# Decode attention over a long cache: thirty units as a hardware loop, each engine in the written order

## The chip, the cores and the metric

The kernel runs on one core of a Trainium2 chip. The metric is the device time of one execution in microseconds (us); runs of one kernel agree within about a tenth of a per cent here.

## The reference

Two branches, mixed by a gate. Cut to what matters:

```python
x = A_x                                              # [2, 1, 1024], bf16
g = sigmoid((x * gate_w).sum(-1, keepdims=True))
# A: attention of one query per head over a cache of 16384 keys
q = (x @ wq) in heads                                # 32 heads of 128
p = softmax(q @ k_cache^T * 128 ** -0.5)             # k_cache, v_cache: [2, 32, 16384, 128]
a = (p @ v_cache) in one row @ wo                    # wo: [4096, 1024]
# B: a small MLP on x (with Sq = 1 the shifted branch hs is zero)
b = x + gelu(layernorm(x) @ w3) @ w4
out = g * a + (1 - g) * b
```

Nearly all of the bytes are the two caches: 2 x 32 x 16384 x 128 x 2 bytes each, 537 MB together. The weights add some 36 MB.

## The kernel before, in words

Two heads of one batch row make a *unit*: 16 pairs of heads (`HP`) times 2 rows (`b`) are 32 units. A unit loads 8.4 MB of K and 8.4 MB of V, each as one DMA of 128 rows of 65,536 bytes. SBUF holds five cells of half such a load in `mem`: K of row 0 takes cells 0 and 1, K of row 1 cells 1 and 2 (they share cell 1), V cells 3 and 4. So a load of K can be issued only when the first half of the K before it, in cell 1, has been used up, and a load of V only when the V before it has.

All large loads are issued by SP's queue, in this order in each pair: K of row 0, V of the row before, K of row 1, V of row 0, with the waits that follow from the shared cells.

What a unit computes:

- `score_first`, `score_second`: K is turned chunk by chunk (8 chunks) by DVE into one of two `KT` buffers (L420), and PE adds the scores up in PSUM, 8 matmuls per chunk (L426). POOL prepares the weights `qw` (L357). The chunks in cell 1 are taken first, so that the next load of K (`load_k`, L108) can start after them.
- `softmax_a`, `softmax_b`: DVE turns the scores (L447) and takes the maximum (L449); ACT (L451) and PE (L457) spread it; ACT takes the exponentials (L464); PE sums them (L475), DVE inverts (L476).
- `pv`: 64 matmuls with V (L492), after which the next V can be loaded (`load_v`, L115).
- `pv_end`: ACT scales (L505), PE gathers (L517), DVE writes the pair's `oT` (L525). After the second row, `project` multiplies `oT` by the pair's two heads of `wo` (L378), held in `wo_pair`, and `load_wo` (L370) fetches the next 512 KB into the same buffer when `project` is through.

The program is software-pipelined by hand: scores of one unit come before the product with V of the unit before. `odd_rest(hp)` finishes unit (hp, 1) and `even_unit(hp + 1)` does unit (hp + 1, 0) and the first half of (hp + 1, 1). They are written out 15 times, which is units 1 to 30; `last_unit` does the rest with its own load of `wo` (`wo_last`, L614) and V in five pieces. A framework schedules this straight-line code: it may move an instruction ahead of others on its engine where the data allow, and it sets the semaphores.

In the trace PE's order differs from the written one in one place: in even units the matmul L457 of `softmax_b` stands before `project`.

Of the kernel before, what the change touches and what calls it, by code (L numbers as in the profile page):

```python
# [23 lines left out]
def kernel(  # L24
# [15 lines left out]
    nc = tc.nc  # L40
# [10 lines left out]
    HP = H // 2  # L51
# [28 lines left out]
    def region(cell, elements, offset=0):  # L80
        at = cell * CELL + offset
        return mem[:, at : at + elements]
# [20 lines left out]
    def cache_rows(cache, hp, b):  # L103
        two = cache[b, bass.ds(2 * hp, 2)]
        return two.rearrange("h s d -> (h s) d").rearrange("(p j) d -> p (j d)", p=P)

    def load_k(hp, b):
        nc.sync.dma_start(out=region(K_CELL[b], NJ * Dh), in_=cache_rows(A_k_cache, hp, b))  # L108

    def load_v(hp, b, cell=V_CELL, pieces=(NJ,)):  # L110
        rows = cache_rows(A_v_cache, hp, b)
        j = 0
        for n in pieces:
            at = slice(j * Dh, (j + n) * Dh)
            nc.sync.dma_start(out=region(cell, NJ * Dh)[:, at], in_=rows[:, at])  # L115
            j += n
# [251 lines left out]
    def load_wo(hp):  # L368
        rows = A_wo[bass.ds(hp * 2 * Dh, 2 * Dh)]
        nc.sync.dma_start(  # L370
            out=wo_pair[:].rearrange("p t n -> p (t n)"),
            in_=rows.rearrange("(p t) n -> p (t n)", p=P),
        )

    def project(oT, weight, last):
        for t in range(2):
            for g in range(Q4):
                nc.tensor.matmul(  # L378
                    arow[QP * g : QP * g + B, :],
                    lhsT=oT[:, t, :],  # L380
                    rhs=weight[:, t, g * G1 : (g + 1) * G1],
                    start=False,
                    stop=(last and t == 1),
                    skip_group_check=True,
                )
# [51 lines left out]
    def score_first(hp, b):  # L437
        write_qw(hp, b)
        score_chunks(b, halves[1 - b], True, False)

    def score_second(b):
        score_chunks(b, halves[b], False, True)

    def softmax_a(b):
        S = S_tiles[b]
        st = ppool.tile([P, GT, QP], FP32, name="St")
        nc.vector.transpose(out=st[:].rearrange("p j r -> p (j r)"), in_=S[:])  # L447
        m = stat.tile([P, 1], FP32, name="m")
        nc.vector.tensor_reduce(out=m[:], in_=st[:, :, 0:NG], axis=AX.XY, op=ALU.max)  # L449
        Dm = ppool.tile([P, P], FP32, name="Dm")  # L450
        nc.scalar.activation(out=Dm[:], in_=ident_s[:], func=ACTF.Copy, scale=m[:, 0:1])  # L451
        st_tiles[b] = (st, Dm)

    def softmax_b(b, by_head=False):
        st, Dm = st_tiles.pop(b)
        R_ps = misc_psum([P, P])
        nc.tensor.matmul(R_ps[:], lhsT=ones_f[:], rhs=Dm[:], start=True, stop=True)  # L457
        nb = stat.tile([P, 1], FP32, name="nb")
        rs = stat.tile([P, 1], FP32, name="rs")
        parts = [slice(e * HALF, (e + 1) * HALF) for e in range(2)]  # L460
        for rows in parts:
            nc.vector.tensor_reduce(out=nb[rows], in_=R_ps[rows, rows], axis=AX.X, op=ALU.min)  # L462
        for e, rows in enumerate(parts):
            nc.scalar.activation(  # L464
                out=pts[b][rows, :, e, :].rearrange("p (m a) k -> p a k m", a=GT // 4),
                in_=st[rows, :, 0:NG].rearrange("p (a k) m -> p a k m", k=4),
                func=ACTF.Exp,
                bias=nb[rows],
                scale=scale,
                accum_out=rs[rows],  # L470
            )
        tot_ps = misc_psum([P, 2])
        rinv = rinvs[b]
        if not by_head:
            nc.tensor.matmul(tot_ps[:, 0:1], lhsT=lmat[:], rhs=rs[:], start=True, stop=True)  # L475
            nc.vector.reciprocal(out=rinv[:, 0:1], in_=tot_ps[:, 0:1])  # L476
        else:
            rs2 = stat.tile([P, 2], FP32, name="rs2")
            nc.vector.tensor_scalar(
                out=rs2[:], in0=hm2[:], scalar1=rs[:, 0:1], scalar2=None, op0=ALU.mult  # L480
            )
            nc.tensor.matmul(tot_ps[:], lhsT=ones_f[:], rhs=rs2[:], start=True, stop=True)
            nc.vector.reciprocal(out=rinv[:], in_=tot_ps[:])
            nc.vector.tensor_scalar(
                out=rinv[:], in0=rinv[:], scalar1=g_rep[:, b : b + 1], scalar2=None, op0=ALU.mult
            )

    def pv(b, g0=0, g1=NJ // 4, ng=NJ // 4, cell=V_CELL):
        V = view(cell)
        for g in range(g0, g1):  # L490
            q = g % Q4
            nc.tensor.matmul(  # L492
                oacc[b][QP * q : QP * q + 8, :],
                lhsT=pts[b][:, g].rearrange("p h k -> p (h k)"),
                rhs=V[:, 4 * g : 4 * g + 4, :].rearrange("p j d -> p (j d)"),
                start=(g < Q4),
                stop=(g >= ng - Q4),
            )
# [12 lines left out]
    def pv_end(b):  # L511
        osb = pv_rows(b, True)[:].rearrange("p (k d t) -> p k t d", k=4, t=2)
        ot = misc_psum([P, 2])
        for t in range(2):
            for k in range(4):
                for h in range(2):
                    nc.tensor.matmul(  # L517
                        ot[h * HALF : (h + 1) * HALF, t : t + 1],
                        lhsT=osb[:, k, t, :],
                        rhs=lane[:, k + 4 * h : k + 4 * h + 1],  # L520
                        start=(k == 0 and t == 0),
                        stop=(k == 3),
                        skip_group_check=True,
                    )
        nc.vector.tensor_scalar(  # L525
            out=oT[:, :, b], in0=ot[:], scalar1=g_rep[:, b : b + 1], scalar2=None, op0=ALU.mult
        )
# [26 lines left out]
    def pv_end_apart(b):  # L554
        osb = pv_rows(b, True)
        ot = misc_psum([P, 2])
        for k in range(4):
            nc.tensor.matmul(
                ot[:], lhsT=osb[:, k * Dh : (k + 1) * Dh], rhs=lane[:, k : k + 5 : 4],
                start=(k == 0), stop=(k == 3),  # L560
            )
        nc.vector.tensor_scalar(
            out=OTl[:, :, b], in0=ot[:], scalar1=g_rep[:, b : b + 1], scalar2=None, op0=ALU.mult
        )
# [14 lines left out]
    softmax_b(0)  # L579

    def odd_rest(hp):
        load_k(hp + 1, 0)
        score_second(1)
        softmax_a(1)
        pv(0)
        load_v(hp, 1)
        pv_end(0)
        softmax_b(1)

    def even_unit(hp):  # L590
        score_first(hp, 0)
        load_k(hp, 1)
        score_second(0)
        softmax_a(0)
        pv(1)
        load_v(hp, 0)
        pv_end(1)
        project(oT, wo_pair, False)
        load_wo(hp)
        softmax_b(0)  # L600
        score_first(hp, 1)

    load_wo(0)
    score_first(0, 1)

    def last_unit(hp):
        V_LAST = 0
        load_v(hp, 1, V_LAST, PIECES)
        score_second(1)
        wo_last = region(V_CELL, 2 * D).rearrange("p (h n) -> p h n", h=2)  # L610
        softmax_a(1)
        pv(0)
        pv_end_apart(0)
        nc.sync.dma_start(  # L614
            out=wo_last, in_=A_wo[(H - 2) * Dh : H * Dh].rearrange("(h d) n -> d h n", d=Dh)
        )
        softmax_b(1, by_head=True)
        pv_last(1, V_LAST)
        project(OTl, wo_last, True)
        nc.vector.tensor_copy(out=out_row[:], in_=arow[:])  # L620
        rows = out.rearrange("b s (g n) -> (b s) g n", g=Q4)
        for b, queue in enumerate((nc.sync, nc.scalar)):
            queue.dma_start(
                out=rows[b], in_=out_row[:].rearrange("(g k) n -> k g n", k=QP)[b]
            )

    LOOPED = False
    if LOOPED:
        with tc.For_i(0, HP - 1, 1, iteration_sync="reg_based") as i:
            odd_rest(i)  # L630
            even_unit(i + 1)
            with tc.If(i >= HP - 2):
                last_unit(HP - 1)
    else:
        for i in range(HP - 1):
            odd_rest(i)
            even_unit(i + 1)
        last_unit(HP - 1)


# [28 lines left out]
```

## Time and profile before

| | |
|---|---|
| three runs | 1343.05, 1343.83, 1343.95 us; median 1343.83 |
| profiled execution | 1342.64 us, of which the span from the first to the last instruction is 1340.8 us |
| busy | PE 755.4, PEld 329.9, DVE 648.7, ACT 129.6, POOL 12.8 us |
| DMA | 573.05 MB read on SP's queue, 428 GB/s on the mean over the span |
| instruction fetches | 45 packets, 0.74 MB on the queue q8; 10 packets, 0.08 MB on q14 |
| mean granted TensorE clock | 0.783 |

Busy times of engines overlap each other; a share of the span says little about what sets the end. In the queues' rows the last number is the time that their packets took, as a share of the time of all 16 DMA engines. "SPq" in the order of time is an issue of a DMA on SP's queue, not the transfer. A bracket at the end of a row is the idle time of the engine before it and what ended that.

### The profile page before, as it was taken

How to read it: one execution, taken by the hardware profiler on the slowest of the kernel's cores; microseconds unless marked ns; L12 is line 12 of the kernel's file. 1: busy time of each engine (PE TensorE's matmuls, PEld its weight loads, DVE VectorE, ACT ScalarE, POOL GpSimd, SP SyncE). 2: the span in 40 equal slices, each digit the busy share in tenths (PEclk: the TensorE clock that was granted, in tenths of full speed). 3: DMA queues.
4: the chain of work that ended last, by engine and by line, in shares of the span. 5: the costliest groups of instructions: out<-in, count | busy, mean ns of one | idle time of the engine just before them, and what ended most of it. 6: DMA issues, size and time to landing. Idle time of an engine off the chain costs nothing.

```text
span 1340.8 us, 12847 instructions
## 1 busy us (share of the span) xinstructions
PE 755.4 (56%) x5758; PEld 329.9 (25%) x5758; DVE 648.7 (48%) x511; ACT 129.6 (10%) x202; POOL 12.8 (1%) x47
## 2 busy tenths in 40 slices
PE   0466555566545466655546655555664555666456
PEld 0222222222222222222222222222222222222223
DVE  1255544455544445554445554444555434455543
ACT  0100011110011111001111101111100111110011
POOL 0000000000000000000000000000000000000000
PEclk9887777888777788776778877778876777887777
DMA  9999999999999999999999999999999999999997
GB/s 407 433 419 438 436 435 423 437 423 438 431 433 436 427 435 431 428 436 435 427 440 435 429 432 423 436 433 437 425 435 433 426 434 421 438 431 440 421 427 316
DMA packets 13575, 573.88 MB, mean 428 GB/s; under 512 B 1864, under 2 KB 1872, under 8 KB 4432
## 3 DMA queue, kind: packets, MB, share of 16 engines
q1 hardware_dynamic: 13096, 573.05, 99.2%
q8 instruction: 45, 0.74, 0.2%
q10 hardware_dynamic: 424, 0.01, 0.0%
q14 instruction: 10, 0.08, 0.0%
HBM read 573.05 MB, written 0.00 MB: 427 GB/s over the span
## 4 chain that ended last, share of the span: by engine, by line
DMA 72%; DVE 12%; PE 12%; issue 4%; POOL 0%; ACT 0%; ACTq 0%; DVEq 0%
DMA mem<-in_A_k_cache_dram 68%; DVE KT L420 11%; PE S L426 11%; DMA gwT<-in_gate_w_dram 2%; DMA mem<-in_A_wo_dram 1%; PE oacc L194 0%; POOL ln_rstd L265 0%; PE misc L259 0%; DVE spread L165 0%; PE misc L245 0%; DVE turn L204 0%; PE arow L378 0%; PE misc L230 0%; ACTq L85 0%; DVE out_row L620 0%
## 5 line engine op out<-in xcount | busy, mean ns | idle before, releaser
L426 PE MATMUL S<-KT,qw 128*128 128x512 bf16 x2048 | 546.3, 416 | 414.4 <-DVE KT L420 414.1
L420 DVE STREAM_TRANSPOSE KT<-mem 128x2048 f32<-128x2048 f32 x256 | 570.6, 2282 | 320.7 <-DMA mem<-in_A_k_cache_dram 270.9
L426 PEld LDWEIGHTS <-qw 128*128 128x128 bf16 x2048 | 218.5, 107 | 737.3 <-issue 557.3
L492 PE MATMUL oacc<-mem,pt 128*8 128x512 bf16 x2032 | 117.0, 383 | 0.3 <-DMA mem<-in_A_v_cache_dram 0.3
L451 ACT ACTIVATE Dm<-ident_s,m 128x128 f32<-128x128 f32 x32 | 12.9, 403 | 1026.5 <-DVE m L449 1026.5
L464 ACT ACTIVATE pt<-St,nb 64x256 bf16<-64x256 f32 x64 | 89.7, 1401 | 61.7 <-DVE nb L462 60.8
L475 PE MATMUL misc<-rs,lmat 128*128 128x1 f32 x62 | 18.2, 362 | 93.4 <-ACT pt L464 93.4
L525 DVE TENSOR_SCALAR oT<-misc,g_rep 128x2 bf16<-128x2 f32 x30 | 6.7, 222 | 129.1 <-PE misc L517 129.1
L492 PEld LDWEIGHTS <-pt 128*8 128x8 bf16 x2032 | 46.6, 87 | 67.8 <-issue 14.8
L447 DVE STREAM_TRANSPOSE St<-S 128x512 f32<-128x512 f32 x32 | 22.9, 717 | 65.8 <-PE S L426 65.8
L476 DVE RECIPROCAL rinv<-misc 128x1 f32<-128x1 f32 x31 | 5.2, 169 | 102.1 <-PE misc L475 102.1
L517 PE MATMUL misc<-lane,osb 128*64 128x1 f32 x960 | 33.8, 199 | 25.5 <-ACT osb L505 25.5
L517 PEld LDWEIGHTS misc<-lane,osb 128*64 128x64 f32 x960 | 31.3, 138 | 40.7 <-ACT osb L505 40.7
L475 PEld LDWEIGHTS misc<-rs,lmat 128*128 128x128 f32 x62 | 15.5, 311 | 101.2 <-ACT pt L464 101.2
L464 ACT ACTIVATION_READ_ACCUMULATOR pt<-St,nb 64x1 f32 x64 | 30.5, 477 | 0.0
L505 ACT ACTIVATE osb<-oacc,rinv 128x512 f32<-128x512 f32 x31 | 21.3, 687 | 58.0 <-PE oacc L492 58.0
L357 POOL TENSOR_TENSOR qw<-qdu,mask 128x16 bf16<-128x16 bf16 x32 | 8.4, 265 | 1184.7 <-PE S L426 1170.5
L462 DVE TENSOR_REDUCE nb<-misc 64x1 f32<-64x64 f32 x64 | 14.2, 222 | 9.2 <-PE misc L457 8.1
L230 PE MATMUL misc<-zp,ones_f 128*128 128x2 f32 x2 | 0.6, 363 | 31.3 <-DVE zp L228 31.3
L457 PE MATMUL misc<-Dm,ones_f 128*128 128x128 f32 x64 | 15.8, 329 | 0.0
L449 DVE TENSOR_REDUCE m<-St 128x1 f32<-128x256 f32 x32 | 13.4, 420 | 1.1
L457 PEld LDWEIGHTS misc<-Dm,ones_f 128*128 128x128 f32 x64 | 9.6, 189 | 0.7 <-issue 0.2
(95 smaller groups left out, 73.7 us busy)
## 6 DMA issues: line engine op xcount, KB each, us to landing
mem<-in_B_w_dram SPq DMA_DIRECT2D x2, 7168.0 KB, 33.0
wo_pair<-in_A_wo_dram SPq DMA_DIRECT2D x16, 512.0 KB, 32.0
mem<-in_B_w_dram SPq DMA_DIRECT2D x2, 2048.0 KB, 10.2
mem<-in_A_v_cache_dram SPq DMA_DIRECT2D x1, 4096.0 KB, 41.6
mem<-in_A_v_cache_dram SPq DMA_DIRECT2D x1, 2048.0 KB, 30.7
mem<-in_A_v_cache_dram SPq DMA_DIRECT2D x1, 1024.0 KB, 29.3
mem<-in_A_v_cache_dram SPq DMA_DIRECT2D x2, 512.0 KB, 28.4
mem<-in_A_k_cache_dram SPq DMA_DIRECT2D x32, 28.7
```

The costliest lines, as they stand in the source:

```text
L420: nc.vector.transpose(out=kt[:], in_=Kc.rearrange("p j d -> p (j d)").bitcast(FP32))
L426: nc.tensor.matmul(S, lhsT=qw[b][:, v, NG - 1 - m : NG - 1 - m + P], rhs=ktb[:, half * GT : (half + 1) * GT, w, :, e], start=(first and n ...
L447: nc.vector.transpose(out=st[:].rearrange("p j r -> p (j r)"), in_=S[:])
L449: nc.vector.tensor_reduce(out=m[:], in_=st[:, :, 0:NG], axis=AX.XY, op=ALU.max)
L451: nc.scalar.activation(out=Dm[:], in_=ident_s[:], func=ACTF.Copy, scale=m[:, 0:1])
L457: nc.tensor.matmul(R_ps[:], lhsT=ones_f[:], rhs=Dm[:], start=True, stop=True)
L462: nc.vector.tensor_reduce(out=nb[rows], in_=R_ps[rows, rows], axis=AX.X, op=ALU.min)
L464: nc.scalar.activation(out=pts[b][rows, :, e, :].rearrange("p (m a) k -> p a k m", a=GT // 4), in_=st[rows, :, 0:NG].rearrange("p (a k) m ...
L475: nc.tensor.matmul(tot_ps[:, 0:1], lhsT=lmat[:], rhs=rs[:], start=True, stop=True)
L492: nc.tensor.matmul(oacc[b][QP * q : QP * q + 8, :], lhsT=pts[b][:, g].rearrange("p h k -> p (h k)"), rhs=V[:, 4 * g : 4 * g + 4, :].rearra ...
L505: nc.scalar.activation(out=osb[:], in_=oacc[b][:], func=ACTF.Copy, scale=rinvs[b][:, 0:1] if scaled else 1.0,)
L517: nc.tensor.matmul(ot[h * HALF : (h + 1) * HALF, t : t + 1], lhsT=osb[:, k, t, :], rhs=lane[:, k + 4 * h : k + 4 * h + 1], start=(k == 0 a ...
```

## The change

The 15 written-out rounds become a loop of the chip's own, in which every engine runs its part of the body and branches back. Three things come with it:

- The loop is made with `iteration_sync="reg_based"`: the engines don't meet between rounds and semaphores are never set back; a wait in the body compares with a register that its engine raises every round.
- `in_order` chains, for each engine, every instruction of the body to the one before it, without a semaphore, so that the schedule keeps the written order. The last unit, in an `If` in the body that holds in the last round alone, is chained in the same way.
- `load_wo` goes from the end of `even_unit` to the head of `odd_rest`, that is, of the body. The first one, ahead of the loop, goes into the first round, and the sixteenth, whose data nothing reads (the last unit has `wo_last`), is gone.

```diff
     def odd_rest(hp):
+        load_wo(hp)
         load_k(hp + 1, 0)
         score_second(1)
 ...
         project(oT, wo_pair, False)
-        load_wo(hp)
         softmax_b(0)
         score_first(hp, 1)
 
-    load_wo(0)
     score_first(0, 1)
 ...
-    LOOPED = False
-    if LOOPED:
-        with tc.For_i(0, HP - 1, 1, iteration_sync="reg_based") as i:
-            odd_rest(i)
-            even_unit(i + 1)
-            with tc.If(i >= HP - 2):
-                last_unit(HP - 1)
-    else:
-        for i in range(HP - 1):
-            odd_rest(i)
-            even_unit(i + 1)
-        last_unit(HP - 1)
+    def in_order():
+
+        last = {}
+        for ins in nc.cur_bb.bb.instructions:
+            if ins.engine in last:
+                tc.add_manual_dep(
+                    ins,
+                    last[ins.engine].name,
+                    mybir.DependencyInfo(
+                        mybir.DependencyClass.NoSync, mybir.DependencyReason.DATA
+                    ),
+                    reason="in order",
+                )
+            last[ins.engine] = ins
+
+    with tc.For_i(0, HP - 1, 1, iteration_sync="reg_based") as i:
+        odd_rest(i)
+        even_unit(i + 1)
+        in_order()
+        with tc.If(i >= HP - 2):
+            last_unit(HP - 1)
+            in_order()
```

## The prediction

> **What bounds it now.** I read the page first, then the stretches of time, the order of time over one pair of heads and over the end, and the DMA packets themselves.
>
> ```profile
> span 1340.8 us, 12847 instructions
> ...
> PE 755.4 (56%) x5758; PEld 329.9 (25%) x5758; DVE 648.7 (48%) x511; ACT 129.6 (10%) x202; POOL 12.8 (1%) x47
> ...
> DMA  9999999999999999999999999999999999999997
> ...
> q1 hardware_dynamic: 13096, 573.05, 99.2%
> q8 instruction: 45, 0.74, 0.2%
> ```
>
> No compute engine is over 56% busy; the DMA engines are at 9 tenths until the last slice.
>
> ```profile
> core 0: us, PE busy (x) PEld busy (x) DVE busy (x) ACT busy (x) POOL busy (x), PEclk, DMA share, GB/s
> 119.00:1284.00 1165.00, 678.87 (x5013) 294.00 (x5011) 584.20 (x415) 114.39 (x177) 7.70 (x29) 0.78 1.00 432
> 1284.00:1341.00 57.00, 31.71 (x270) 14.63 (x270) 21.09 (x19) 7.00 (x11) 0.00 (x0) 0.73 0.83 355
> ```
>
> In the 1165 us of the thirty units the DMA share is 1.00. A packet of 65,536 bytes takes 2.42 us on its engine and the next begins where it ends. So time there is bytes, not waits; what an engine loses off the DMA counts only past its cover. The cover is seen in one odd unit:
>
> ```profile
> 750.53 0.33 SPq L108 DMA_DIRECT2D mem<-in_A_k_cache_dram  x1
> ...
> 752.75 1.90 PE L426 MATMUL S<-KT,qw 128*128 128x512 bf16 x8 [0.29 <-DVE KT L420]
> ...
> 764.82 0.33 SPq L115 DMA_DIRECT2D mem<-in_A_v_cache_dram  x1
> ...
> 766.69 0.49 PE L457 MATMUL misc<-Dm,ones_f 128*128 128x128 f32 x2
> ...
> 781.34 4.51 DVE L420 STREAM_TRANSPOSE KT<-mem 128x2048 f32<-128x2048 f32 x2 [10.19 <-DMA mem<-in_A_k_cache_dram]
> ```
>
> V is issued at 764.8 while K still runs until 774.5 on the earliest DMA engine and 780.9 on the latest; then DVE sits 10.2 us until K is in.
>
> **A hidden spread.** Each load is eight large packets and one 4-byte packet on each of 16 engines. The 4-byte packets of the load that ended at 166.4 us lie within 1.8 us of each other; of the one that ended at 1018.4, within 7.9: seven engines within 1.8 us of the first, nine 4.1 to 7.9 behind. Over ten rounds (four loads and one wo each) the earliest engine goes from 164.5 to 951.2, 78.67 us a round, and the latest from 166.4 to 957.8, 79.14. What differs is the q8 row: PE's instructions come as 45 packets of 16,384 bytes, one per 256 instructions (11,516 matmuls and weight loads), each 1.07 us on one DMA engine; followed from end to start they take about eight engines in rotation. A buffer is full when its latest engine is done, so those engines pace the kernel, 0.47 us a round behind the bytes.
>
> **The change, part by part.** The sum starts from the profiled execution, 1342.64 us (span 1340.80, 1.84 around it); the median of three runs, 1343.83, is 1.19 above.
>
> *One load of wo less.* It is 512 KB: at 16 x 65,536 bytes per 2.42 us, 1.21 us. It is issued at 1283.77, ahead of the last V pieces:
>
> ```profile
> 1283.77 0.33 SPq L370 DMA_DIRECT2D wo_pair<-in_A_wo_dram  x1
> 1284.15 22.96 SPq L115 DMA_DIRECT2D mem<-in_A_v_cache_dram  x5
> ...
> 1330.67 1.04 PE L492 MATMUL oacc<-mem,pt 128*8 128x512 bf16 x16 [0.34 <-DMA mem<-in_A_v_cache_dram]
> ...
> 1336.87 0.60 PE L378 MATMUL arow<-mem,OTl 128*2 128x256 bf16 x8 [0.70 <-DMA mem<-in_A_wo_dram]
> ```
>
> The end waits for DMA there three times, 0.34, 0.74 (last V piece) and 0.70 us, and the earlier two sum to 1.08 before the compute chain is the end itself: gain 1.1.
>
> *Load of wo at the head.* On SP nothing stands between the old and the new place: V, wo, K, V, K, V, wo is the queue either way, and wo's wait for project (2.35 us each, 35.3 over 15) still ends some 21 us before the next K is issued (729.32, 750.53). Zero; without that cover, a few tenths.
>
> *Written order.* Against the order of time only one pair swaps: the maximum's matmul L457 (728.47) now stands behind project (728.89), which waits for oT. softmax_b starts some 0.8 us later in even units, under DVE's 7.1 us wait for K at 740.0. Zero; uncovered, 15 x 0.8.
>
> *The loop, instructions.* A round is 336 matmuls and 336 weight loads (163 and 172 matmuls in two 39-us stretches): 2.6 packets of 256. The arm with the last unit, jumped over in 14 rounds, holds 236 of each, 1.85 packets. A round's path on PE thus spans about 4.5 packets. If they stay in PE's instruction memory, the loop fetches nothing after its first round. Then the latest DMA engine loses its lag: at least 2.63 / 8 x 1.07 = 0.35, at most 0.47 us a round, over 15 rounds 5.3 to 7.1; I take 6.2. If each round fetches anew the sign turns (first rival). What speaks for staying is the rotation over eight DMA engines, eight packets under way or in place against 4.5 needed; it is inference, and no run here has a loop. [...]
>
> *The loop, waits and branches.* Waits compare with registers, and every engine takes two taken branches a round: over the last unit's arm, and back. No row shows either. Nearest rows: 0.02 to 0.06 us between a KT's end and its matmul; for a missed fetch, 1.25 us (output issue 1337.98 to packet 1339.22) plus none or one large packet of 2.42 plus 1.07: 2.3 to 4.7 us a branch, 9.4 a round. PE's back edge falls after 752.5, ahead of V's issue, whose cover is 774.5 - 764.8 - 1.25 = 8.5 us to the earliest DMA engine and 14.8 to the latest. SP, ACT and POOL have over 20 us between their uses. Zero in the rounds. In the last round the handovers from K's landing (1295.4) to the output are bare: about 25 steps, none to 0.05 each, 0 to 1.2 us; I take 0.7. There a lost fetch would be bare too, 4.7 at most.
>
> *Entering the loop.* SP may have to see the loads ahead of the loop land before it issues its first K in the loop. That K is issued at 118.44 now; the loads land from 124.6 on the earliest engine to 127.7 on the latest. Then the latest engine stands for 1.25 us, the earliest for 127.7 + 1.25 - 124.6 = 4.4, their middle 3, once. Zero to 3; I take 1.5, near the latest engine's.
>
> Sum: 1342.64 - 1.1 - 6.2 + 0.7 + 1.5 = 1337.5; on the median, **1338.7**. With the ends of each term 1335.6 (7.1 saved, nothing paid) to 1346.3 (5.3 saved; 1.2, 4.7 and 3 paid).
>
> **Rivals.**
> *PE's instructions are fetched anew each round: slower.* Place: PE's two taken branches. A path of 4.5 packets with the one ahead at both jumps is 6 a round against 2.63. Spread over eight engines, 6 / 8 x 1.07 = 0.80 us a round against 0.47 now: +5; if a block always comes over the same engine, 1.07 a round, +9. With -1.1, +0.7, +1.5: 1350 to 1354, call it 1350. It decides where fewer than five packets stay in place; the break-even is about 3.5 fetched a round. For it: the 45 packets come one per 256 instructions, as two places used in turn would give as well. Against: the eight engines. [...]
> *As many fetches as now.* 2 to 4 packets a round, say because the arm stays but the body doesn't: only wo is left, minus tail and entry: 1343 to 1345, no change. The rotation speaks no more for this than for a full refetch.
> *A stall past its cover.* Two misses behind a queue as deep as at the start (small packets for gate_w took 29.6 us there) hold PE over 15 us; every us beyond costs 15: 1365 with 1.5 over. In the steady part PE's fetches begin within 7 us of the instruction that crosses the block, so this is unlikely.
>
> **How the numbers follow.** Forecast 0.50, full refetch 0.33, fetches as now 0.10, stall past cover 0.07. A difference under 0.2% (2.7 us) can't be told from none. Of the forecast's 0.50, 0.03 falls within 2.7 us through the entry and tail terms; the case of equal fetches gives 0.08 to no change, 0.02 to slower. So faster 0.47, same 0.11, slower 0.42. The range holds the forecast from its low end (1335.6, with 1 below for the fetches of the other engines, 10 packets now) to the refetch on fixed engines, 1354; left out are the stall case, 0.07, and some of the edges. The forecast's own range is 1334.5 to 1346.3.
>
> **What would show it.** Right: q8 in the changed profile falls from 45 to about 10 packets; q1 falls from 573.05 to 572.53 MB; the spread between the DMA engines' last packets stays under 3 us through the loop; DMA share stays 1.00; SP keeps V, wo, K. Wrong: q8 at 75 or more packets, with the spread growing faster than 0.47 us a round; DMA share under 0.98 in the rounds with SP waiting; PE idle at L426 put down to issue after the first half's matmuls; or a gap in DMA at 120 to 130 us well over 3 us.

## The result and the profile after

The changed kernel takes 1408.37 us (median of 4 runs, 1406.83 to 1413.45) against 1343.44 beside it: 1.049 times the time of before, with a 95% interval of 1.0462 to 1.0519. It is slower by 65 us, 4.6 us for each of the 14 rounds that pass over the last unit. Its four runs lie 0.5% apart, those of the kernel before 0.1%. The forecast was 1338.7 in a range of 1334.5 to 1354; it was wrong, in sign and in size.

The profiled execution took 1406.83 us. Its page, in the rows that answer to those shown of before:

```profile
span 1404.7 us, 14848 instructions
...
DMA  9999999989899998999989898998989999898996
...
q1 hardware_dynamic: 12952, 572.53, 95.3%
q8 instruction: 7, 0.11, 0.0%
...
wo_pair<-in_A_wo_dram SPq DMA_DIRECT2D x15, 512.0 KB, 3.3
```

The last of these rows, in the page of before:

```profile
wo_pair<-in_A_wo_dram SPq DMA_DIRECT2D x16, 512.0 KB, 32.0
```

The part that I forecast a gain from is there: q8 has 7 packets where there were 45, and q1 carries 0.52 MB less. But the DMA row now has an 8 every few slices (a round is 2.4 of them): the DMA engines run dry. The row of wo says where. The median wo now lands 3.3 us after its issue, where it took 32.0 before: it used to stand in a queue of work, and now meets an empty one. The one issued at 729.32 before had its first packet at 753.90; the one issued at 706.12 now has it at 707.19, and its packets, eight of 4,096 bytes on each of the 16 DMA engines at 0.16 us each, are through at 709.10.

From SP's part of the order of time, two rounds (start, duration, engine and line, operation, tile and source):

```profile
672.85 0.33 SPq L115 DMA_DIRECT2D mem<-in_A_v_cache_dram  x1
706.12 0.33 SPq L370 DMA_DIRECT2D wo_pair<-in_A_wo_dram  x1
706.96 0.34 SPq L108 DMA_DIRECT2D mem<-in_A_k_cache_dram  x1
...
756.55 0.33 SPq L115 DMA_DIRECT2D mem<-in_A_v_cache_dram  x1
790.66 0.33 SPq L370 DMA_DIRECT2D wo_pair<-in_A_wo_dram  x1
```

Between V at 672.85, the last issue of one body, and wo at 706.12, the first of the next, SP issues nothing for 33 us. The 4-byte packets that end the load of V land between 703.87 and 704.68 us, and nothing is queued behind it. Before, wo and K went out while V was still on its way:

```profile
726.60 0.33 SPq L115 DMA_DIRECT2D mem<-in_A_v_cache_dram  x1
729.32 0.33 SPq L370 DMA_DIRECT2D wo_pair<-in_A_wo_dram  x1
750.53 0.33 SPq L108 DMA_DIRECT2D mem<-in_A_k_cache_dram  x1
```

There this V's last packets end between 753.9 us on the earliest DMA engine and 760.0 on the latest, so K stood in the queue 3.4 to 9.5 us before them, behind wo. The DMA engines over the edge of the changed kernel, by stretches (the last three columns are granted clock, DMA share and GB/s):

```profile
core 0: us, PE busy (x) PEld busy (x) DVE busy (x) ACT busy (x) POOL busy (x), PEclk, DMA share, GB/s
703.00:709.00 6.00, 5.42 (x24) 2.22 (x23) 4.34 (x2) 0.00 (x0) 0.00 (x0) 1.00 0.47 175
709.00:716.00 7.00, 5.39 (x100) 2.83 (x98) 1.45 (x4) 1.09 (x2) 0.27 (x1) 1.00 0.84 337
716.00:728.00 12.00, 0.59 (x2) 0.53 (x3) 0.52 (x3) 2.81 (x4) 0.00 (x0) 0.51 1.01 437
```

In the thirteen microseconds from 703 to 716 the DMA lost 0.53 x 6 + 0.16 x 7 = 4.3 us; from 716 on it is full. The longest wait of SP's queue (waiting line, what it waited for: us in total, times, longest):

```profile
SPq L645 <- SPq L645: 441.3, 28, 19.6
```

L645 is the `If` around the last unit. SP waits there 28 times, twice in each of the 14 rounds that jump over it, for 441 us, and the row of the profile doesn't say for whom. The records of the trace do. These are SP's records of L645 behind the branch at the edge above: start, operation, and the semaphore that it waits for (`>=`) and then raises (`+=`):

```
673.53 ALU_OP
673.62 EVENT_SEMAPHORE  $S[115]>= $S[115]+=
673.69 ALU_OP
673.76 EVENT_SEMAPHORE  $S[116]>= $S[116]+=
673.83 ALU_OP
673.90 EVENT_SEMAPHORE  $S[117]>= $S[117]+=
673.96 ALU_OP
685.72 EVENT_SEMAPHORE  $S[118]>= $S[118]+=
685.79 ALU_OP
705.07 EVENT_SEMAPHORE  $S[119]>= $S[119]+=
705.14 EVENT_SEMAPHORE  $S[120]>= $S[120]+=
705.21 EVENT_SEMAPHORE  $S[121]>= $S[121]+=
705.28 EVENT_SEMAPHORE  $S[122]>= $S[122]+=
```

The trace has these instructions, eight in each of the 14 rounds (17 ns each once the wait is over):

```profile
L645 SPq EVENT_SEMAPHORE  x112: 17/17/17, 173.8 to 1292.8; - x112
```

By the issues' records, loads take eight semaphores in turn, 115 to 122 in the trace and counted 0 to 7 here. In the body wo has 0, K of row 0 has 1, V of the row before 2, K of row 1 has 3, V of row 0 has 4; the eight DMAs of the arm (V in five pieces, wo_last, two outputs) go on with 5, 6, 7, 0, 1, 2, 3, 4. In each of the 14 rounds that jump over the arm SP raises all eight by hand, as I read it so that they stand as if the arm had run, and the raise waits first: in all 14 rounds that of 3 comes 0.02 us after the last count of K of row 1, and that of 4 comes 0.02 us after the last count of V of row 0. In the edge above, three of them are raised by 673.96, the one of K of row 1 at 685.72 and the one of V of row 0 at 705.07. V's last packet had landed at 704.68, and V's semaphore had its last count at 705.05. Only then come a branch at 705.58, wo at 706.12 and the next K at 706.96. In the 14 rounds it is 33.0 to 34.6 us from V to wo, and 1.9 us from V's last count to the next K: each time, every load that the body had issued had landed before the next body issued one.

### The profile page after: what moved, and what is told of

It is laid out like the page before. It is cut to its first block, busy times and chain, and to the rows that moved or that the text cites. A ratio compares the mean times of both kernels' runs of the same rounds, so it can differ in the third digit from the quotient of the medians.

```text
span 1404.7 us, 14848 instructions
## 1 busy us (share of the span) xinstructions
PE 765.4 (54%) x5758; PEld 334.5 (24%) x5758; DVE 651.5 (46%) x511; ACT 129.6 (9%) x202; POOL 12.8 (1%) x47
## 5 line engine op out<-in xcount | busy, mean ns | idle before, releaser
L426 PE MATMUL S<-KT,qw 128*128 128x512 bf16 x2048 | 553.1, 421 | 437.1 <-DVE KT L420 429.7
L475 PE MATMUL misc<-rs,lmat 128*128 128x1 f32 x62 | 18.2, 362 | 100.7 <-ACT pt L464 55.1
L457 PE MATMUL misc<-Dm,ones_f 128*128 128x128 f32 x64 | 17.4, 357 | 0.0
L457 PEld LDWEIGHTS misc<-Dm,ones_f 128*128 128x128 f32 x64 | 10.7, 210 | 4.1 <-issue 3.9
```

The costliest lines, as they stand in the source:

```text
L426: nc.tensor.matmul(S, lhsT=qw[b][:, v, NG - 1 - m : NG - 1 - m + P], rhs=ktb[:, half * GT : (half + 1) * GT, w, :, e], start=(first and n ...
```

## The experiments

Three theories stood after the result, and the expectations number them so. Theory 1 (landing): this wait of SP on the path past the arm. Theory 2 (edge): what every loop brings, its branch back and its waits on registers. Theory 3 (order): the written order delays the issue of K.

**The last unit behind the loop.** There is no arm here, and so there are no semaphores to raise; the rest of the loop is as changed.

```diff
-        with tc.If(i >= HP - 2):
-            last_unit(HP - 1)
-            in_order()
+    last_unit(HP - 1)
```

> The loop of 15 rounds stays, with the written order and the load of wo at its head; the last unit stands after the loop, so that there is no arm to jump over. Theory 1 (landing): on the path past the arm SP raises the semaphores of the arm's eight loads by hand and waits for each to stand at the value of the last load that used it, so K and V must have landed at each round's edge; the DMA engines run dry some 4.4 us in each of 14 rounds. Without the arm the rounds run at the rate of the bytes, 1336 us, and leaving the loop costs once, since SP sees all loads land there: 1336 + 3 to 10 = 1339 to 1346. Theory 2 (edge): the branch back and the waits on registers cost by themselves, in every round, arm or not: 1400 to 1410. Theory 3 (order): the written order delays K's issue: 1400 to 1410.

It took 1344.55 us (1344.07 to 1346.12), 1.0011 of before [1.0002, 1.0021]. The loss is gone, with the loop, its branch back, the register waits and the written order still there: theories 2 and 3 fall. But it isn't faster than before either. Leaving the loop costs once nearly what each round cost, 0.71 x 5 = 3.6 us of DMA against the 4.3 at the edge above:

```profile
1295.00:1305.00 10.00, 5.38 (x23) 2.07 (x21) 3.93 (x2) 0.00 (x0) 0.00 (x0) 0.99 1.03 446
1305.00:1310.00 5.00, 1.57 (x13) 0.41 (x13) 1.50 (x1) 0.00 (x0) 0.00 (x0) 0.54 0.29 84
```

The DMA share falls to 0.29 for these 5 us. SP stood at L641, the line of the loop, until a V landed, before it issued V of the last unit:

```profile
SPq L641 <- DMA mem<-in_A_v_cache_dram: 8.8, 1, 8.8
```

**One load less in the arm.** V of the last unit in four pieces of 128, 64, 32, 32 columns instead of five; all else as changed. By the count above the arm's seven loads end at semaphore 3, so 4, that of V, is not raised.

```diff
-    PIECES = (128, 64, 32, 16, 16)
+    PIECES = (128, 64, 32, 32)
```

> The changed kernel with the arm's last two V pieces (16 and 16) joined in one of 32, so that the arm has seven loads in place of eight; nothing else. The eight load semaphores go round: wo 0, K 1, V 2, K 3, V 4 in the body, and the arm goes on with 5, 6, 7, 0, 1, 2, 3; the one that falls out is 4, that of the V issued last. Theory 1 (landing): SP waits past the arm for K alone (semaphore 3), which lands some 10 us before SP could issue its next K anyway, and no longer for V: 1335 to 1341, some 68 us less than the changed kernel, from one load joined. Theories 2 and 3: no change but the last piece, 1405 to 1412.

It took 1339.23 us (1338.45 to 1342.51), 0.9974 [0.9964, 0.9983]: 69.1 us less than the change, for two pieces joined in one line of the last unit: 4.9 for each of the 14 rounds that pass the arm. It also beats the kernel before, by 0.3%.

```profile
span 1336.1 us, 14788 instructions
...
DMA  9999999999999999999999999999999999999997
...
q8 instruction: 7, 0.11, 0.0%
```

The row of DMA is at 9 throughout. In its order of time wo goes out 14 us after V and the next K 11 us later, and V is still being read then (its last packets land at 1148.6 to 1150):

```profile
1117.87 0.33 SPq L115 DMA_DIRECT2D mem<-in_A_v_cache_dram  x1
1132.30 0.34 SPq L370 DMA_DIRECT2D wo_pair<-in_A_wo_dram  x1
1143.77 0.33 SPq L108 DMA_DIRECT2D mem<-in_A_k_cache_dram  x1
```

SP still stands at L645, once a round instead of twice, now for K alone:

```profile
SPq L645 <- SPq L645: 165.7, 15, 12.5
```

These 165.7 us of waiting cost nothing, because K lands a whole V, 19 us, before the DMA would run dry. In the edge shown, K's semaphore has its last count at 1131.23 us, SP raises it at 1131.25, and wo goes out 1.05 us later.

**Two loads less.** `PIECES = (128, 64, 64)`, so that K's semaphore isn't raised either.

> As the run with seven loads in the arm, but V in three pieces (128, 64, 64): six loads in the arm, and semaphore 3 (K) falls out too. Theory 1: the wait for K was free, so the same as with seven, plus up to 1.5 us for 64 single matmuls after the last piece, in place of 32: 1335 to 1343. If the wait for K also held something back, it is faster than with seven by more than 2 us. Theories 2 and 3: 1405 to 1412.

It took 1340.48 us (1338.52 to 1341.9), 0.9978 [0.9968, 0.9988]: no difference from seven that the intervals would show. Of the 165.7 us at L645 one wait is left:

```profile
SPq L645 <- SPq L645: 0.3, 1, 0.3
```

The wait for K was covered, and of the two waits it is V's landing alone that costs.

**The same wait without a loop.** To see whether that wait is enough by itself, I wrote the rounds out again, in the written order and with wo at the head, and gave SP a small transfer out of V's cell ahead of each wo, at which SP waits until V has landed (L585, 14 times, 463.2 us in the row below).

```diff
     def odd_rest(hp):
+        if hp:
+            nc.sync.dma_start(out=probe[0:1], in_=region(V_CELL, 2)[0:1])
         load_wo(hp)
```

First without the transfer, which prices the written order and the moved wo alone:

> No loop: the 15 rounds written out as before, but each chained in the written order, the load of wo at the head, and the last pair's wo loaded once. Theories 1 and 2: the order is free (the one pair that swaps lies under DVE's wait for K) and one 512 KB load less gives 1.1 us: 1341 to 1343.5. PE's instructions come as some 45 packets again. Theory 3: 1400 to 1410.

It took 1342.09 us (1341.62 to 1342.69), 0.9989 [0.9979, 0.9999], with 45 packets on q8: 1.3 under before, which fits one wo less (the interval allows 0.1 to 2.8). Then with it:

> No loop and no arm: the 15 rounds written out in the written order, with one thing added. Ahead of each load of wo but the first, SP issues a copy of 4 bytes out of the V cell into a tile that nothing reads, so SP waits there until the V issued last has landed. Theory 1 (landing): this wait alone is the price. The loop with eight loads in its arm takes 69 us more than with seven, 4.9 a round; here SP has about 1 us less to do between the landing and the next loads (no registers, no branches), so 3 to 4.6 us in each of 14 rounds on top of 1342: 1384 to 1406. Theory 2 (edge: the wait costs only together with the loop's own steps): 1342 to 1346.

It took 1397.23 us (1396.63 to 1398.72), 1.0402 [1.0384, 1.0419]: 55.1 us over the kernel without it, 3.9 a round in 14 rounds.

```profile
DMA  9999989999899899989989999998999999899998
...
SPq L585 <- DMA mem<-in_A_v_cache_dram: 463.2, 14, 34.9
```

The DMA row has the same 8s, with no loop and no branch. The loop pays 1 us a round more. Most of that lies between V's last packet and the issue of the next K, where the loop has raises, branch and register work: 2.3 us there (2.2 to 2.4 over the 14 rounds), 1.4 here (1.4 to 1.8).

**What the loop is worth.** Joining two pieces changes the tail as well. So I ran the written-out rounds of e3 once more, now in four pieces:

```diff
-    PIECES = (128, 64, 32, 16, 16)
+    PIECES = (128, 64, 32, 32)
```

> No loop: the rounds written out in the written order, wo moved, and V of the last unit in four pieces as in e2_arm7. e3_unrolled_order is the same with five pieces: 1342.09 us; e2_arm7 the same inside the loop: 1339.23. Question: how much of e2's 2.9 us under e3 is the loop (instruction fetches gone) and how much the shape of the tail. If the joined piece costs nothing or little, 1341.5 to 1343.5 with 45 packets on q8, and the loop's gain is 2.3 to 4.3 us; if the tail in four pieces is itself the gain, 1339 to 1340 and the loop is worth nothing. My first theory (step: fetches are the pacing of the latest DMA engine) expects the former.

It took 1341.85 us (1341.35 to 1343.58), 0.9992 [0.9983, 1.0001]; five pieces gave 0.9989. The joined piece is worth nothing by itself, and the loop in e2 is worth 2.6 us (0.9974 against 0.9992, two intervals that just touch). That is less than the 6.2 that I gave for the fetches, though the gain in landing arrives in full: the last engine lands the last unit's K at 1288.18 us in e2 and at 1295.22 here, 7.0 earlier. The rest is lost in the tail. Here, without a loop (PE's sums over the last V, then DVE's step on them):

```profile
1334.73 1.01 PE L548 MATMUL misc<-pt,mem 128*128 128x2 bf16 x32 [0.42 <-DMA mem<-in_A_v_cache_dram]
1335.78 0.16 DVE L552 TENSOR_TENSOR OTl<-misc,rinv 128x2 bf16<-128x2 f32 x1 [8.09 <-PE misc L548]
```

And in e2, where this code is within the loop (64 matmuls in one row; `remote` is a release that the profile can put down to no engine):

```profile
1326.63 2.27 PE L548 MATMUL misc<-pt,mem 128*128 128x2 bf16 x64
1330.64 0.16 DVE L552 TENSOR_TENSOR OTl<-misc,rinv 128x2 bf16<-128x2 f32 x1 [10.38 <-remote]
```

DVE starts 0.04 us after PE's end in the first and 1.74 us in the second. In the loop, each of the 64 matmuls and 64 weight loads of L548 raises PE's semaphore by one; in e10, as in the kernel before, only the last of the 64 matmuls raises it. The semaphore's record in the trace of e2 shows the 128 raises one by one, 30 ns apart, the last at 1330.62, 0.02 us before DVE starts; PE was through with the 128 instructions in 2.27 us, at 1328.90. The changed kernel's trace has the same: PE is through at 1397.53, the last raise is at 1399.24, and DVE starts at 1399.27. The e1 kernel supports this: its last unit is behind the loop, one raise serves its 64 matmuls, and there the lag is 0.04 us. Another 1.0 us stands at the very end: from the output's issue to the end of the span it is 4.0 us in e2 and 3.0 here, and in e2 the branches and semaphore waits of leaving the loop lie between.

**A longer body.** Does PE's code stay in place because the loop is short? Three pairs in a body, five rounds, about ten packets of instructions; the seven loads in the arm.

```diff
-    with tc.For_i(0, HP - 1, 1, iteration_sync="reg_based") as i:
-        odd_rest(i)
-        even_unit(i + 1)
+    with tc.For_i(0, HP - 1, 3, iteration_sync="reg_based") as i:
+        for d in range(3):
+            odd_rest(i + d)
+            even_unit(i + d + 1)
```

(`qw` is written by DVE here instead of POOL, and the `If` asks for `i >= HP - 4`.)

> The loop with seven loads in the arm, but with three pairs of heads in the body and five rounds; DVE writes qw in place of GpSimd, 0.3 us each. SP still waits for no V past the arm. PE's path round the loop grows from 4.5 to about 10 packets of 256 instructions. Theory A (the loop's instructions stay in PE's memory of eight packets): ten no longer fit, the q8 queue shows 45 or more packets, the DMA engines spread apart again, and most of the gain over the unrolled order goes: 1341 to 1347. Theory B (once in a loop PE fetches nothing however long the body is): q8 at 16 to 20 packets (one pass through a longer program), 1338 to 1340.

It took 1349.38 us (1347.7 to 1350.18), 1.0046 [1.003, 1.0063]. The fetches are back:

```profile
q8 instruction: 54, 0.88, 0.3%
```

From the first edge on, each of the bodies that follow fetches ten packets. The DMA engines drift apart again too: the spread of K's last packets goes from 2.3 us at 184 us to 3.9 at 341, before the first edge (1.8 to 3.4 in the kernel before, 1.8 to 1.5 in e2). The time is over what I expected, though, and the order of time at an edge of the loop shows why:

```profile
363.20 4.50 DVE L420 STREAM_TRANSPOSE KT<-mem 128x2048 f32<-128x2048 f32 x2 [7.39 <-PEq L646]
363.21 0.33 SPq L108 DMA_DIRECT2D mem<-in_A_k_cache_dram  x1
366.55 5.78 PE L426 MATMUL S<-KT,qw 128*128 128x512 bf16 x15 [8.79 <-issue]
```

PE stands 8.8 us for nothing but issue, with packets on q8 at 360.3, 363.6 and 369.8; the next K can't be issued until 363.21, while V began to land at 360.57. Rounds without an edge take 78.6 us here and the two edges that I followed 81.8 and 81.1. It is the rival of the prediction, a stall past its cover, in a kernel that fetches anew. The eight packets of theory A were inferred from the DMA engines that the fetches went round in the kernel before; the runs show only that 4.5 stayed and ten did not.

**Without the chained order**, the loop of e2 with the `in_order` calls left out:

> The loop with seven loads in the arm, without the chain that keeps the written order. The schedule then puts a part of the matmuls with V of row 0 at the head of the body, ahead of the scores' second half, where that V has some 9 us to land still. If the written order is what makes the loop good: PE waits there each round, DVE's KT and the next V stand behind it, and what goes over the cover of about 15 us is paid 15 times: 1345 to 1385. If the order in the loop is free as it is written out: 1337 to 1341.

It took 1347.21 us (1346.52 to 1348.92), 1.0035 [1.002, 1.0049], 8 us over e2. The time is at the low end of what I expected, but the loss is not in the rounds, where I expected it: their GB/s are near those of e2. In the last slice of the span it has 188 GB/s against 298, and SP's last wait grows from 21.7 us to 32.5. In the last unit, PE's order of time has this row:

```profile
1307.10 1.86 PE L492 MATMUL oacc<-mem,pt 128*8 128x512 bf16 x13 [6.16 <-DMA mem<-in_A_v_cache_dram]
```

The schedule has put 13 of the matmuls with V of row 0 ahead of the last 32 of the scores. PE stands 6.2 us for this V, the scores wait behind it, and the maximum's matmul L457 runs at 1323.65 us instead of 1315.30 in e2; the span is 8.7 us longer. So the written order mattered in the last unit alone.

**The last unit's order**, tried on e2: the maximum's matmul L457 and the exponentials ahead of `pv(0)`, the row totals behind it. `row_before` holds `pv(0)`, `pv_end_apart(0)` and the load of `wo_last`.

```diff
         softmax_a(1)
-        pv(0)
-        pv_end_apart(0)
 ...
-        softmax_b(1, by_head=True)
+        softmax_b(1, by_head=True, between=row_before)
```

> The loop with seven loads in the arm, and in the last unit another order: PE takes the maximum's matmul L457 ahead of the 64 matmuls with V of row 0 and what follows them, so that the exponentials of row 1 run beside them. In the run with seven loads the DMA engines were done at 1327.5 us and the end waited for the compute chain; L457 stood ready at 1311.3 and ran at 1315.3. If the chain is the end there, 2 to 4 us less than with seven: 1335 to 1337. If the end is the last V piece and the work behind it: 1338 to 1340.

It took 1338.92 us (1337.52 to 1339.97), 0.9969 [0.9958, 0.998]: not told apart from e2, so what the shorter chain is worth is too small to see. The last piece of V (0.31 us of waiting before the sums over it, L550 in this kernel) and the same lag of 1.74 us behind PE's raises set the end, not the stretch that I had shortened.

## Why the prediction was wrong, point by point

**The step that failed** is "The loop, waits and branches", and in it the sentence that "SP, ACT and POOL have over 20 us between their uses. Zero in the rounds." That step weighed a branch only as a missed fetch, at up to 4.7 us, and set it beside SP's idle time. I left out what SP does here on the side of the `If` that isn't taken, eight raises behind waits. SP has its 20 us, but spends them, and more, on a wait whose end is the landing of the V that it has just issued: 33 us from V to wo. Zero became 4.9 us a round, 69.1 in all by e2, and e6 shows that the wait is enough without a loop (3.9 a round).

The "Entering the loop" term had the mechanism in hand: "SP may have to see the loads ahead of the loop land before it issues its first K in the loop." I priced it once, at the loop's head, and didn't ask it of the round's edge. At the head it cost nothing measurable: K's landings follow the load ahead by 145.52 - 124.92 = 20.60 us after and 145.19 - 124.62 = 20.57 before. At the exit, in e1, it is there, 8.8 us at L641 for a V.

**The rival that came nearest**, the stall past its cover (0.07, 1365), had the form right, as what went past the cover was paid round by round (4.9 us in each of 14), but put it on PE's missed fetches. And the sign "DMA share under 0.98 in the rounds with SP waiting" was named in the last paragraph, without a mechanism, a price or a chance.

**One load of wo less:** 1.1 forecast, 1.3 by e3, within an interval of 0.1 to 2.8. **The written order, and wo at the head:** zero forecast in the rounds, and e3 leaves nothing for them to have cost. In the changed kernel project stands ahead of the maximum's matmul in even units, and no transfer waits for it:

```profile
758.83 0.39 PE L378 MATMUL arow<-wo_pair,oT 128*2 128x256 bf16 x8 [0.35 <-DVE oT L525]
759.15 0.49 PE L457 MATMUL misc<-Dm,ones_f 128*128 128x128 f32 x2
```

**The loop's instructions:** right in mechanism and size. q8 falls to 7 packets; in e2 the spread between the DMA engines' last packets stays at 1.5 to 1.6 us for each K from the second round on, a round takes 78.69 us, which is the earliest engine's 78.67 of before, and the last K lands 7.0 us earlier than in e10 (5.3 to 7.1 forecast). The refetch rival (0.33) falls for this body, and e7 shows that it is real for one of about ten packets. A path of about 4.5 packets with two taken branches a round fetched 7 packets in the whole kernel, the last at 201.3 us in the changed one. No run shows the six fetches a round that the rival's 1350 was added up from.

**The handovers in the last round** were put at 0.7 (0 to 1.2). That term was too small: of the 7.0 us that K gained over e10, the span gained 4.0 (1340.1 to 1336.1) and the medians some 2.6. 1.7 of the lost 3.0 in the span is the lag behind PE's raises, and 1.0 is the end of the loop behind the output's issue. I had taken the handover per step; the large one went by the number of PE's instructions ahead of it, 128 raises at 30 ns.

With the wait gone, the sum that I made came out within a microsecond: 1339.23 for e2 against 1338.7. Two of its errors cancel in that (entry 1.5 against none; the tail 0.7 against some 3), so the closeness is in part luck.

## What to carry to other kernels

In this loop, SP raised the eight semaphores of the arm by hand in each of the 14 rounds that jumped over it, and waited at them for the body's loads that shared them. In a loop built like this one, count the DMAs in the arm and see whose semaphores they come round to. In a kernel whose DMA share is 1.00 through its units, the issue held until the load ahead had landed was paid in every round, 4.9 us, though SP had over 20 us between its uses; so when you price a branch, price the waits on both its sides. And when code is rolled into a loop, count PE's instructions between the two jumps in blocks of 256: here a loop of four or five blocks fetched nothing after 203 us, and one of ten fetched ten in each body and stalled at its edge.

## What the runs showed of the hardware that was not expected

- The time hangs on the number of DMAs in an arm that the round jumps over: eight instead of seven cost 69 us, seven instead of six nothing that the runs could tell, because the eighth falls on the semaphore of V.
- In the loop, PE's semaphore goes up by one per matmul and weight load of L548, 30 ns apart, slower than PE gets through them (128 in 2.27 us): for this burst of 64 and 64, DVE starts 1.74 us after PE's end, in the changed kernel and in e2. In the rounds a lag is there too, after pv (V issued 4.19 us after its first matmul, 752.36 to 756.55, against 3.67 before), and covered.
- Instruction packets cost more than their share of the time says. They take 0.2% of the DMA engines' time and, on about half of the engines, set back the landing of the loads by up to 6 us at the end (e10: a spread of 7.3 us, against 1.6 in e2). Taking them away brought the last K in 7.0 us earlier.
